# Row order of wo in its buffer, the turning of the attention quotients, and the place of the last gather, in a gated mix of cached attention and a GeGLU FFN

## The chip, the cores and the metric

The kernel runs on one core of one Trainium2 chip. The metric is device microseconds (us) of one execution; a lower number is better. A kernel is run several times and the median is compared. Beside these times one execution is recorded by the hardware profiler; its rows give start and duration of every instruction on TensorE (PE, with its weight loads as PEld), VectorE (DVE), ScalarE (ACT), GpSimd (POOL) and on the queue of SyncE (SPq), which issues all the transfers of this kernel.

## What is computed

Four decode tokens `x` (4 x 512) go through two branches that a gate mixes. Branch a is attention over a cache of 4096 keys for 32 heads of 128; branch b is a GeGLU feed-forward network of width 1792. All data is float32.

```python
g = sigmoid((x * gate_w).sum(-1, keepdims=True))
q = (x @ wq) as (4, 32, 1, 128)
scores = einsum("bhqd,bhkd->bhqk", q, k_cache) * 128 ** -0.5
o = einsum("bhqk,bhkd->bhqd", softmax(scores), v_cache)
a = o as (4, 1, 4096) @ wo                      # wo: 4096 x 512
b = (gelu(x @ w_gate) * (x @ w_up)) @ w_down    # w_down: 1792 x 512
out = g * a + (1 - g) * b
```

k_cache and v_cache are 268 MB each, and every byte is read once. wq and wo are 8.4 MB each, and the three FFN matrices 3.7 MB each.

## The kernel before

**Tiles and the loop.** The work is cut into 64 steps (`for i in range(NT)`, L311). Step i handles one pair of heads `g = i // 4` for one batch row `b = i % 4`. Its keys are one tile of 128 partitions x 32 KB (4096 KB): 64 partitions for each of the two heads, and in each partition 64 consecutive keys, so that partition p holds bytes that lie in memory right behind those of partition p-1. Its values have the same form. Five such buffers (`NB = 5`, pool `kv`) hold all large loads in turn: the two halves of wq, keys, values, w_gate, w_up, w_down and the two halves of wo (`load`, L61).

**The order of loads.** A list (L82 to L87) fixes it: keys one step ahead of values, and at the end k63, wo's first half ("w0"), v61, v62, v63 (in two halves), w_down ("d0"), and wo's second half ("w1", in three pieces of 10, 4 and 2 of its 16 blocks, `WO_END`). `load_next()` issues the next of the list on the SP queue at three places of a step: behind `sums(i)`, behind `pv(i - 1)`, and in step 62 behind `project_a(0)`. Each load waits until the buffer that it takes has been read for the last time. So k63 and w0 are issued in step 60, v61 and v62 in step 61, v63, d0 and w1 in step 62.

**A step.** VectorE multiplies the keys by the query in two halves (`products`, L192) and sums over the head's 128 elements (`sums`, L196). `max_a` (L203, L205) takes each partition's maximum and transposes it on TensorE. In the next step, between the two halves of `products`, `soft_max` reduces it (L210), spreads it by a matmul (L212), and ScalarE takes the exponentials (L217) into a zero-padded buffer. Then `pv` (L235) multiplies them by the values, 16 matmuls accumulating in PSUM over the four batch rows of a pair.

**Behind each pair.** `gather(g)` copies PSUM by ScalarE (L244), sums by four matmuls (L247), and adds the softmax's denominators by another (L249); the sums stand as 8 rows (batch, head of the pair) x 128. `weigh(g)` takes the reciprocal (L256) and writes the quotients into one of eight places of the buffer `ONA` (L257).

**Behind 8 pairs.** Once for each half of wo (step 33, and the end of the kernel) the quotients of 16 heads must become columns, with the contraction over wo's 2048 rows on 128 partitions in 16 blocks `e`. `turn(w)` does it by 32 matmuls (L265): for each of the two heads of a pair and each e, a weight block of 8 x 64 against a selecting matrix `hsel`. `turned(w)` copies the result to SBUF by ScalarE (L272). The partition that a quotient comes to is (head of the pair, k, pair): this is why wo's rows are loaded out of order. `project_a(w)` then is 64 matmuls against wo (L228), 4 for each block e; `project` places the four quarters of the output on four groups of 32 partitions.

wo's load before (L77 to L80) takes the rows of one half as `(g s e)`, with g = 8 pairs, s = 16 and e = 16, and puts row block (g, s) into partition 8 s + g. Each partition gets 16 consecutive rows, 32 KB, but neighbouring partitions of the same s lie 256 rows (512 KB) apart in memory.

**The end.** Behind the loop (L345 to L359) the order is: `soft_max(63)`, `pv(63)`, `ffn_down(0, 5)` (20 of w_down's 56 matmuls), `gather(15)`, `ffn_down(5, 9)`, `weigh(15)`, `turn(1)`, `turned(1)`, `ffn_down(9, 14)`, `project_a(1)`, the gated sum (L358), and the store of the output. Each engine works through its instructions in the order in which they are written. A fp32 matmul stands in the profile as two records, a transpose as one. The transfers of all loads go through the same queue, whose 16 DMA engines the profile shows as one share.

Of the kernel before, what the change touches and what calls it, by code (L numbers as in the profile page):

```python
# [9 lines left out]
F32 = mybir.dt.float32  # L10
AF = mybir.ActivationFunctionType
OP = mybir.AluOpType
AX = mybir.AxisListType
# [4 lines left out]
def tile_gated_mix(ctx: ExitStack, tc: tile.TileContext, x, kc, vc, wq, wo, w_gate, w_up, w_down, gate_w, out):  # L18
    nc = tc.nc
    P = 128  # L20
    B, H, S, D = kc.shape
    DM = x.shape[2]
# [3 lines left out]
    HT = 2  # L26
    PH = P // HT
# [8 lines left out]
    FC = F // P  # L36
    HW = 16
    E = HW * D // P
# [5 lines left out]
    head = ctx.enter_context(tc.tile_pool(name="head", bufs=1))  # L44
    ident = head.tile([P, P], F32)
    ones = head.tile([P, P], F32)
    sel = head.tile([P, RJ, B, HT], F32)
    hsel = head.tile([B * HT, HT, B, 8], F32)
    qd = head.tile([P, D], F32)
    xT = head.tile([P, KC, 4, B, 8], F32)  # L50
    kv = ctx.enter_context(tc.tile_pool(name="kv", bufs=NB))
    consts = ctx.enter_context(tc.tile_pool(name="consts", bufs=1))
    work = ctx.enter_context(tc.tile_pool(name="work", bufs=2))
    ps2 = ctx.enter_context(tc.tile_pool(name="ps2", bufs=2, space=PSUM))
    ps1 = ctx.enter_context(tc.tile_pool(name="ps1", bufs=1, space=PSUM))
# [5 lines left out]
    def load(kind, i):  # L61
        t = T[kind, i] = kv.tile([P, TW], F32, name="kv")
        if kind in "kv":
            h, b = HT * (i // B), i % B
            src = (kc if kind == "k" else vc)[b, h:h + HT].rearrange("h (p r) d -> (h p) (r d)", p=PH)
            n = 2 if (kind, i) == ("v", NT - 1) else 1
            for s in range(n):
                nc.sync.dma_start(t[:, s * TW // n:(s + 1) * TW // n], src[:, s * TW // n:(s + 1) * TW // n])
        elif kind == "q":
            nc.sync.dma_start(t, wq.rearrange("(p c) n -> p (c n)", c=KC)[:, i * TW:(i + 1) * TW])  # L70
        elif kind == "f":
            nc.sync.dma_start(t[:, :KC * F], (w_gate, w_up)[i].rearrange("(p c) n -> p (c n)", c=KC))
        elif kind == "d":
            nc.sync.dma_start(t[:, :FC * DM], w_down.rearrange("(p i) n -> p (i n)", i=FC))
        else:

            src = wo[i * HW * D:(i + 1) * HW * D].rearrange("(g s e) n -> s g (e n)", s=HT * D // E, e=E)  # L77
            ends = WO_END if i else (0, E)
            for e0, e1 in zip(ends, ends[1:]):
                nc.sync.dma_start(t[:, e0 * DM:e1 * DM], src[:, :, e0 * DM:e1 * DM])  # L80

    loads = [("q", 0), ("q", 1), ("k", 0)]  # L82
    for i in range(NT - 2):
# [6 lines left out]
    def load_next():  # L90
        n = next(loads, None)
        if n:
            load(*n)
# [13 lines left out]
    for j in range(RJ):  # L107
        nc.vector.tensor_reduce(sel[:, j], ident.rearrange("p (c b m) -> p b m c", c=4, b=B)[:, :, HT * j:HT * (j + 1), :],
                                axis=AX.X, op=OP.add)

    for h in range(HT):
        nc.vector.tensor_copy(hsel[:, h], ident[:B * HT, h:B * HT:HT][:, :, None].to_broadcast([B * HT, B, 8]))


    PZ = 32 - RJ * HT
# [30 lines left out]
    for c in range(KC):  # L146
        w = T["q", c // 2].rearrange("p (c n) -> p c n", c=2)[:, c % 2, :]
# [7 lines left out]
    m16 = consts.tile([P, 4 * B], F32)  # L155
    bmask = consts.tile([P, B], F32)
    amask = consts.tile([P, HG], F32)
    hmask = consts.tile([P, 4, HG], F32)
    nc.vector.tensor_reduce(m16, ident.rearrange("p (m a) -> p m a", a=HG), axis=AX.X, op=OP.add)
    nc.vector.tensor_reduce(bmask, m16.rearrange("p (j b) -> p b j", b=B), axis=AX.X, op=OP.add)  # L160
    nc.vector.tensor_reduce(amask, ident.rearrange("p (m a) -> p a m", a=HG), axis=AX.X, op=OP.add)
    nc.vector.tensor_reduce(hmask, ident.rearrange("p (j b a) -> p j a b", j=4, b=B), axis=AX.X, op=OP.add)
    for s in range(2):
# [5 lines left out]
                            op=OP.mult)  # L169
# [56 lines left out]
    def project(acc, t, w, start, stop):  # L226
        for c in range(4):
            nc.tensor.matmul(acc[32 * c:32 * c + 32, :], t, w[:, c * C4:(c + 1) * C4], start=start, stop=stop)  # L228

    def pv(i, j0=0, j1=R // RJ):  # L230
        g, b = divmod(i, B)
        N, n = RJ * D, R // RJ
        for j in range(j0, j1):
            c, m0 = j % 4, PZ + 32 * j - RJ * HT * b
            nc.tensor.matmul(PO[g % 2][32 * c:32 * c + 32].rearrange("p j d -> p (j d)"), PM[i % 2][:, m0:m0 + 32],  # L235
                             T["v", i][:, j * N:(j + 1) * N], start=b == 0 and j < 4, stop=b == B - 1 and j >= n - 4)
# [3 lines left out]
    OS, OT = {}, {}  # L240

    def gather(g):
        o = work.tile([P, RJ, D], F32, name="o", bufs=1)
        nc.scalar.activation(o, PO[g % 2], AF.Copy)  # L244
        OS[g] = ps2.tile([B * HT, D + 1], F32, name="sm")
        for j in range(RJ):
            nc.tensor.matmul(OS[g][:, :D], sel[:, j].rearrange("p b h -> p (b h)"), o[:, j, :],  # L247
                             start=j == 0, stop=j == RJ - 1)
        nc.tensor.matmul(OS[g][:, D:], RS[g % 2].rearrange("p b h -> p (b h)"), ones[:, :1], start=True, stop=True)  # L249


    ONA = consts.tile([B * HT, E, D // E, HW // HT], F32)

    def weigh(g):
        ri = work.tile([B * HT, 1], F32, name="ri")
        nc.vector.reciprocal(ri, OS[g][:, D:])  # L256
        nc.vector.tensor_scalar(ONA[:, :, :, g % (HW // HT)], OS[g][:, :D].rearrange("p (k e) -> p e k", e=E), ri, None,  # L257
                                op0=OP.mult)


    def turn(w):
        OT[w] = ps1.tile([P, E, 32], F32, name="oT")
        for h in range(HT):
            for e in range(E):
                nc.tensor.matmul(OT[w][h * PH:(h + 1) * PH, e, :], ONA[:, e].rearrange("p k g -> p (k g)"),  # L265
                                 hsel[:, h].rearrange("p b k -> p (b k)"), start=True, stop=True)

    OTS = {}

    def turned(w):  # L270
        OTS[w] = work.tile([P, E, 32], F32, name="ot", bufs=1)
        nc.scalar.activation(OTS[w], OT[w], AF.Copy)  # L272

    def project_a(w, e0=0, e1=E):
        for e in range(e0, e1):
            project(a_acc, OTS[w][:, e, :], T["w", w][:, e * DM:(e + 1) * DM], (w, e) == (0, 0),
                    (w, e) == (H // HW - 1, E - 1))

# [22 lines left out]
        for i in range(FC):  # L301
            nc.vector.transpose(hT[:, i, :], v[:, i::FC])

    def ffn_down(i0, i1):
        w = T["d", 0].rearrange("p (f n) -> p f n", n=DM)
        for f in range(i0, i1):
            project(b_acc, hT[:, f, :], w[:, f, :], f == 0, f == FC - 1)


# [1 line left out]
    for i in range(NT):  # L311
        g, b = divmod(i, B)
# [4 lines left out]
        if pair:  # L317
            weigh(g - 1)
# [9 lines left out]
        if pair and g % (HW // HT) == 0:  # L328
            turn(g // (HW // HT) - 1)
            turned(g // (HW // HT) - 1)  # L330
# [11 lines left out]
        if i == NT - 2:  # L342
            project_a(0)
            load_next()
    soft_max(NT - 1)  # L345
    pv(NT - 1)
    ffn_down(0, 5)
    gather(H // HT - 1)
    ffn_down(5, 9)
    weigh(H // HT - 1)  # L350
    turn(H // HW - 1)
    turned(H // HW - 1)
    ffn_down(9, FC)
    tb = consts.tile([P, C4], F32)
    nc.vector.tensor_scalar(tb, b_acc, g_cols[:, 1:2], None, op0=OP.mult)
    project_a(H // HW - 1)
    res = work.tile([P, C4], F32, name="res")
    nc.vector.scalar_tensor_tensor(res, a_acc, g_cols[:, 0:1], tb, op0=OP.mult, op1=OP.add)  # L358
# [23 lines left out]
```

## Time and profile before

| | |
|---|---|
| time, median of 3 runs | 1342.33 us (1341.08 to 1342.93) |
| time of the profiled execution | 1340.75 us |
| span of the profiled execution, first to last instruction | 1339.0 us |
| granted TensorE clock, mean over the span | 0.652 |
| busy: VectorE / TensorE / ScalarE | 87% / 38% / 7% of the span |
| HBM read over the span | 564.67 MB, 422 GB/s |
| DMA queue of the loads | busy for 99.5% of the span on 16 engines |

A row of a group or of the timeline names the line of the code, the engine, the operation, the written and the read tile, the shapes and the count (x). Behind it stands in brackets how long the engine had been idle and what ended that. "xN" in the timeline are N instructions drawn together. A row of stretches gives for each engine the busy time in it, then the granted TensorE clock as a share of full speed, the busy share of the DMA engines, and what they moved. Times of the timeline count from the start of the span.

### The profile page before, as it was taken

How to read it: one execution, taken by the hardware profiler on the slowest of the kernel's cores; microseconds unless marked ns; L12 is line 12 of the kernel's file. 1: busy time of each engine (PE TensorE's matmuls, PEld its weight loads, DVE VectorE, ACT ScalarE, POOL GpSimd, SP SyncE). 2: the span in 40 equal slices, each digit the busy share in tenths (PEclk: the TensorE clock that was granted, in tenths of full speed). 3: DMA queues.
4: the chain of work that ended last, by engine and by line, in shares of the span. 5: the costliest groups of instructions: out<-in, count | busy, mean ns of one | idle time of the engine just before them, and what ended most of it. 6: DMA issues, size and time to landing. Idle time of an engine off the chain costs nothing.

```text
span 1339.0 us, 7575 instructions
## 1 busy us (share of the span) xinstructions
PE 506.5 (38%) x3100; PEld 174.4 (13%) x3100; DVE 1162.4 (87%) x399; ACT 90.3 (7%) x359; POOL 0.7 (0%) x6
## 2 busy tenths in 40 slices
PE   3143334243324342443245243424433342443146
PEld 1011111011101011111022111101111110111014
DVE  2999999999997699899999999999999899999830
ACT  0000000000000000000000000000000000000000
POOL 0000000000000000000000000000000000000000
PEclk9656676676667656665675666567666666666577
DMA  9999999999999999999999999999999999999997
GB/s 407 438 423 438 435 426 437 433 429 437 432 430 437 428 435 435 427 436 434 429 436 432 430 436 433 429 438 432 430 436 430 433 434 432 432 436 431 290 396 210
DMA packets 20077, 565.15 MB, mean 422 GB/s; under 512 B 2360, under 2 KB 2376, under 8 KB 2508
## 3 DMA queue, kind: packets, MB, share of 16 engines
q1 hardware_dynamic: 20044, 564.69, 99.5%
q8 instruction: 24, 0.39, 0.1%
q14 instruction: 9, 0.07, 0.0%
HBM read 564.67 MB, written 0.01 MB: 422 GB/s over the span
## 4 chain that ended last, share of the span: by engine, by line
DMA 60%; DVE 37%; PE 2%; issue 1%; ACT 0%; SPq 0%; DVEq 0%; ACTq 0%
DMA kv<-in_A_k_cache 53%; DVE kv L192 18%; DVE sc L196 18%; DMA kv<-in_A_v_cache 3%; DMA kv<-in_A_wo 3%; DMA kv<-in_A_wq 2%; PE po L235 0%; DVE m L203 0%; PE po L151 0%; DVE m L210 0%; PE q L286 0%; PE a_acc L228 0%; DVE ONA L257 0%; PE sm L205 0%; PE q L180 0%
## 5 line engine op out<-in xcount | busy, mean ns | idle before, releaser
L192 DVE TENSOR_TENSOR kv<-kv,qb 128x4096 f32<-128x4096 f32 x128 | 564.9, 4414 | 78.4 <-DMA kv<-in_A_k_cache 76.6
L196 DVE TENSOR_REDUCE sc<-kv 128x64 f32<-128x8192 f32 x64 | 555.9, 8686 | 6.3
L235 PE MATMUL po<-kv,pm 128*32 128x512 f32 x2048 | 365.0, 877 | 297.3 <-DMA kv<-in_A_v_cache 291.4
L235 PEld LDWEIGHTS po<-kv,pm 128*32 128x32 f32 x2048 | 91.2, 154 | 515.7 <-issue 507.6
L212 PE MATMUL sm<-m,ones 1*128 1x2 f32 x128 | 37.0, 356 | 319.7 <-DVE m L210 319.7
L205 PE MATMUL sm<-ident,m 128*1 128x128 f32 x64 | 18.9, 296 | 176.6 <-DVE m L203 176.5
L212 PEld LDWEIGHTS sm<-m,ones 1*128 1x128 f32 x128 | 31.5, 304 | 351.0 <-DVE m L210 343.7
L214 ACT ACTIVATE nb<-sm 128x2 f32<-128x2 f32 x64 | 11.0, 172 | 815.3 <-PE sm L212 815.3
L217 ACT ACTIVATE pm<-sc,nb 64x64 f32<-64x64 f32 x128 | 44.6, 348 | 2.9
L210 DVE TENSOR_REDUCE m<-sm 1x2 f32<-1x128 f32 x64 | 17.4, 272 | 27.3 <-PE sm L205 27.3
L205 PEld LDWEIGHTS sm<-ident,m 128*1 128x1 f32 x64 | 5.1, 79 | 224.1 <-issue 121.1
L180 PE MATMUL q<-QM,hmask 128*64 128x512 f32 x64 | 24.3, 848 | 3.4 <-DVE QM L168 3.4
L184 ACT ACTIVATE qb<-q 128x512 f32<-128x512 f32 x16 | 9.6, 597 | 226.0 <-PE q L180 226.0
L217 ACT ACTIVATION_READ_ACCUMULATOR pm<-sc,nb 64x1 f32 x128 | 23.6, 185 | 0.0
L247 PE MATMUL sm<-o,sel 128*8 128x128 f32 x128 | 17.2, 279 | 10.7 <-ACT o L244 10.7
L244 ACT ACTIVATE o<-po 128x512 f32<-128x512 f32 x16 | 9.6, 597 | 138.5 <-PE po L235 138.5
L203 DVE TENSOR_REDUCE m<-sc 128x1 f32<-128x64 f32 x64 | 14.1, 220 | 2.2
L256 DVE RECIPROCAL ri<-sm 8x1 f32<-8x1 f32 x16 | 2.3, 147 | 15.2 <-PE sm L249 15.2
L247 PEld LDWEIGHTS sm<-o,sel 128*8 128x8 f32 x128 | 10.6, 92 | 26.8 <-ACT o L244 24.6
L151 PE MATMUL po<-kv,xT 128*32 128x512 f32 x64 | 10.9, 846 | 3.1 <-DMA kv<-in_A_wq 2.7
L164 DVE TENSOR_TENSOR u<-po,amask 128x512 f32<-128x512 f32 x2 | 1.4, 692 | 11.5 <-PE po L151 11.5
L265 PE MATMUL oT<-hsel,ONA 8*64 8x32 f32 x128 | 10.6, 257 | 0.0
(50 smaller groups left out, 88.3 us busy)
## 6 DMA issues: line engine op xcount, KB each, us to landing
kv<-in_A_k_cache SPq DMA_DIRECT2D x64, 4096.0 KB, 39.8
kv<-in_A_v_cache SPq DMA_DIRECT2D x63, 4096.0 KB, 30.6
kv<-in_A_wq SPq DMA_DIRECT2D x2, 4096.0 KB, 16.5
kv<-in_A_wo SPq DMA_DIRECT2D x1, 4096.0 KB, 53.8
kv<-in_A_v_cache SPq DMA_DIRECT2D x2, 2048.0 KB, 41.7
kv<-in_B_w_gate SPq DMA_DIRECT2D x1, 3584.0 KB, 38.6
kv<-in_B_w_up SPq DMA_DIRECT2D x1, 3584.0 KB, 28.2
kv<-in_B_w_down SPq DMA_DIRECT2D x1, 3584.0 KB, 26.0
```

What stands on the lines that cost most here:

```text
L151: nc.tensor.matmul(PO[s][32 * j:32 * j + 32].rearrange("p j d -> p (j d)"), xT[:, c, :32], w[:, n0:n0 + HB * D], start=c == 0, stop=c == K ...
L180: nc.tensor.matmul(ps[h * PH:(h + 1) * PH].rearrange("p b d -> p (b d)"), hmask[:, j, a:a + 1].to_broadcast([P, PH]), QM.rearrange("p b d ...
L192: nc.vector.tensor_tensor(t, t, QB[g][:, b:b + 1, :].to_broadcast([P, r1 - r0, D]), op=OP.mult)
L196: nc.vector.tensor_reduce(SC[i], T["k", i].rearrange("p (r d) -> p r d", d=D), axis=AX.X, op=OP.add)
L203: nc.vector.tensor_reduce(m1, SC[i], axis=AX.X, op=OP.max)
L205: nc.tensor.transpose(MT[i], m1, ident)
L210: nc.vector.tensor_reduce(m2, MT[i].rearrange("o (h p) -> o h p", h=HT), axis=AX.X, op=OP.max)
L212: nc.tensor.matmul(nbp, ones[:1, :], m2, start=True, stop=True)
L214: nc.scalar.activation(nb, nbp, AF.Copy, scale=-scale)
L217: nc.scalar.activation(PM[i % 2][:, PZ:].rearrange("p (c m) -> p c m", m=32)[s, :, h:RJ * HT:HT], SC[i][s, :].rearrange("p (c j) -> p c j" ...
L235: nc.tensor.matmul(PO[g % 2][32 * c:32 * c + 32].rearrange("p j d -> p (j d)"), PM[i % 2][:, m0:m0 + 32], T["v", i][:, j * N:(j + 1) * N], ...
L247: nc.tensor.matmul(OS[g][:, :D], sel[:, j].rearrange("p b h -> p (b h)"), o[:, j, :], start=j == 0, stop=j == RJ - 1)
```

## The change

There are three edits. wo's rows go into the buffer in their order in memory: partition p takes rows 16 p to 16 p + 15 of the half, so that the contraction's partition is (pair, head of the pair, k). For this `weigh` writes every quotient twice, once for each head of the pair (8 x 256 elements instead of 8 x 128), `turn` transposes the 8 x 128 blocks by 16 PE transposes instead of 32 matmuls, and `turned` multiplies the result by a mask that keeps in each partition the columns of its own head (`pmask`, from `m16`, once), adds the two columns, and spreads the sum to 8 equal columns by ScalarE. The two copies into `hsel` at the start go. And at the end of the kernel all of w_down's matmuls stand behind `gather`, `weigh`, `turn` and `turned`, where they stood in three parts in front of and between them.

```diff
-    hsel = head.tile([B * HT, HT, B, 8], F32)
+    t1 = head.tile([P, E * B], F32)
...
-            src = wo[i * HW * D:(i + 1) * HW * D].rearrange("(g s e) n -> s g (e n)", s=HT * D // E, e=E)
+            src = wo[i * HW * D:(i + 1) * HW * D].rearrange("(p e) n -> p (e n)", e=E)
             ends = WO_END if i else (0, E)
             for e0, e1 in zip(ends, ends[1:]):
-                nc.sync.dma_start(t[:, e0 * DM:e1 * DM], src[:, :, e0 * DM:e1 * DM])
+                nc.sync.dma_start(t[:, e0 * DM:e1 * DM], src[:, e0 * DM:e1 * DM])
...
-    for h in range(HT):
-        nc.vector.tensor_copy(hsel[:, h], ident[:B * HT, h:B * HT:HT][:, :, None].to_broadcast([B * HT, B, 8]))
...
+    pmask = consts.tile([P, HT], F32)
...
+    nc.vector.tensor_reduce(pmask, m16.rearrange("p (g h) -> p h g", h=HT), axis=AX.X, op=OP.add)
...
-    ONA = consts.tile([B * HT, E, D // E, HW // HT], F32)
+    ONA = consts.tile([B * HT, E, HW // HT, HT, D // E], F32)
...
-        nc.vector.tensor_scalar(ONA[:, :, :, g % (HW // HT)], OS[g][:, :D].rearrange("p (k e) -> p e k", e=E), ri, None,
-                                op0=OP.mult)
+        nc.vector.tensor_scalar(ONA[:, :, g % (HW // HT)],
+                                OS[g][:, :D].rearrange("p (k e) -> p e k", e=E)[:, :, None, :]
+                                .to_broadcast([B * HT, E, HT, D // E]), ri, None, op0=OP.mult)
...
     def turn(w):
-        OT[w] = ps1.tile([P, E, 32], F32, name="oT")
-        for h in range(HT):
-            for e in range(E):
-                nc.tensor.matmul(OT[w][h * PH:(h + 1) * PH, e, :], ONA[:, e].rearrange("p k g -> p (k g)"),
-                                 hsel[:, h].rearrange("p b k -> p (b k)"), start=True, stop=True)
+        OT[w] = ps1.tile([P, E, B, HT], F32, name="oT")
+        for e in range(E):
+            nc.tensor.transpose(OT[w][:, e].rearrange("p b h -> p (b h)"), ONA[:, e].rearrange("q g h k -> q (g h k)"),
+                                ident[:B * HT, :B * HT])
...
     def turned(w):
+        t = work.tile([P, E * B, HT], F32, name="tm", bufs=1)
+        nc.vector.tensor_tensor(t, OT[w].rearrange("p e b h -> p (e b) h"),
+                                pmask[:, None, :].to_broadcast([P, E * B, HT]), op=OP.mult)
+        nc.vector.tensor_tensor(t1, t[:, :, 0], t[:, :, 1], op=OP.add)
         OTS[w] = work.tile([P, E, 32], F32, name="ot", bufs=1)
-        nc.scalar.activation(OTS[w], OT[w], AF.Copy)
+        nc.scalar.activation(OTS[w].rearrange("p e (b k) -> p (e b) k", k=8), t1[:, :, None].to_broadcast([P, E * B, 8]),
+                             AF.Copy)
...
     soft_max(NT - 1)
     pv(NT - 1)
-    ffn_down(0, 5)
     gather(H // HT - 1)
-    ffn_down(5, 9)
     weigh(H // HT - 1)
     turn(H // HW - 1)
     turned(H // HW - 1)
-    ffn_down(9, FC)
+    ffn_down()
```

Nothing else of the loop, of the order of loads or of the sizes of transfers changes; wo's second half still comes in three pieces, each of all 128 partitions.

More of the change, by code (lines that the diff above doesn't have):

```diff
@@ L256, in weigh, with project_a @@
         nc.vector.reciprocal(ri, OS[g][:, D:])
-        nc.vector.tensor_scalar(ONA[:, :, :, g % (HW // HT)], OS[g][:, :D].rearrange("p (k e) -> p e k", e=E), ri, None,
-                                op0=OP.mult)
+        nc.vector.tensor_scalar(ONA[:, :, g % (HW // HT)],
+                                OS[g][:, :D].rearrange("p (k e) -> p e k", e=E)[:, :, None, :]
+                                .to_broadcast([B * HT, E, HT, D // E]), ri, None, op0=OP.mult)
     def turn(w):
-        OT[w] = ps1.tile([P, E, 32], F32, name="oT")
-        for h in range(HT):
-            for e in range(E):
-                nc.tensor.matmul(OT[w][h * PH:(h + 1) * PH, e, :], ONA[:, e].rearrange("p k g -> p (k g)"),
-                                 hsel[:, h].rearrange("p b k -> p (b k)"), start=True, stop=True)
+        OT[w] = ps1.tile([P, E, B, HT], F32, name="oT")
+        for e in range(E):
+            nc.tensor.transpose(OT[w][:, e].rearrange("p b h -> p (b h)"), ONA[:, e].rearrange("q g h k -> q (g h k)"),
+                                ident[:B * HT, :B * HT])
     OTS = {}
     def turned(w):
+        t = work.tile([P, E * B, HT], F32, name="tm", bufs=1)
+        nc.vector.tensor_tensor(t, OT[w].rearrange("p e b h -> p (e b) h"),
+                                pmask[:, None, :].to_broadcast([P, E * B, HT]), op=OP.mult)
+        nc.vector.tensor_tensor(t1, t[:, :, 0], t[:, :, 1], op=OP.add)
         OTS[w] = work.tile([P, E, 32], F32, name="ot", bufs=1)
-        nc.scalar.activation(OTS[w], OT[w], AF.Copy)
-    def project_a(w, e0=0, e1=E):
-        for e in range(e0, e1):
+        nc.scalar.activation(OTS[w].rearrange("p e (b k) -> p (e b) k", k=8), t1[:, :, None].to_broadcast([P, E * B, 8]),
+                             AF.Copy)
+    def project_a(w):
+        for e in range(E):
             project(a_acc, OTS[w][:, e, :], T["w", w][:, e * DM:(e + 1) * DM], (w, e) == (0, 0),
@@ L302, in ffn_gelu, with ffn_down @@
             nc.vector.transpose(hT[:, i, :], v[:, i::FC])
-    def ffn_down(i0, i1):
+    def ffn_down():
         w = T["d", 0].rearrange("p (f n) -> p f n", n=DM)
-        for f in range(i0, i1):
+        for f in range(FC):
             project(b_acc, hT[:, f, :], w[:, f, :], f == 0, f == FC - 1)
```

## The prediction

> **What bounds the kernel now.** I read the chain of waits first, then the costliest groups, then stretches of the end.
>
> ```profile
> DMA 60%; DVE 37%; PE 2%; issue 1%; ACT 0%; SPq 0%; DVEq 0%; ACTq 0%
> ...
> L192 DVE TENSOR_TENSOR kv<-kv,qb 128x4096 f32<-128x4096 f32 x128 | 564.9, 4414 | 78.4 <-DMA kv<-in_A_k_cache 76.6
> ```
>
> VectorE is busy, but 76.6 us of its idle time ends with keys that land: over 64 steps 1.2 us per step are left over. The loop runs at the pace of the transfers. So I ask how fast these run, in stretches (the last two columns are the DMA engines' busy share and GB/s):
>
> ```profile
> 1200.00:1245.00 45.00, 17.01 (x97) 5.32 (x89) 40.95 (x15) 2.69 (x11) 0.00 (x0) 0.69 1.01 434
> 1250.00:1275.00 25.00, 0.00 (x0) 0.00 (x0) 16.45 (x4) 0.63 (x4) 0.00 (x0) 0.50 0.99 215
> 1278.00:1290.00 12.00, 2.88 (x16) 0.91 (x20) 0.00 (x0) 0.00 (x0) 0.00 (x0) 0.50 1.01 434
> 1295.00:1309.00 14.00, 6.80 (x109) 3.43 (x97) 12.10 (x4) 1.54 (x8) 0.00 (x0) 0.87 1.02 435
> 1311.00:1329.00 18.00, 13.39 (x182) 9.60 (x178) 0.60 (x2) 0.85 (x2) 0.00 (x0) 0.78 0.95 217
> ```
>
> Twice the rate falls to half, 215 and 217 GB/s, while the engines stay busy: the queue isn't empty, its packets are slow. The issues tell what moves then. Keys land a median of 39.8 us after their issue and values 30.6 us:
>
> ```profile
> kv<-in_A_k_cache SPq DMA_DIRECT2D x64, 4096.0 KB, 39.8
> kv<-in_A_v_cache SPq DMA_DIRECT2D x63, 4096.0 KB, 30.6
> ```
>
> ```profile
> 1223.80 0.66 SPq L80 DMA_DIRECT2D kv<-in_A_wo  x1
> ...
> 1243.17 0.34 SPq L68 DMA_DIRECT2D kv<-in_A_v_cache  x1
> ...
> 1262.03 0.80 SPq L68 DMA_DIRECT2D kv<-in_A_v_cache  x2
> ...
> 1293.12 0.33 SPq L74 DMA_DIRECT2D kv<-in_B_w_down  x1
> ```
>
> w0 is issued at 1223.80, so it moves some 25 to 50 us later: the first slow stretch. The second begins when w1's turn comes. v63's halves, w_down and all keys run at 434 between. The only load with rows out of memory order is wo. What the slow stretches cost stands in the chain from 1244 us on:
>
> ```profile
> 1243.17 43.81 DMA kv<-in_A_v_cache
> ...
> 1287.12 5.94 PE po L235 x32
> ...
> 1293.27 3.63 PE a_acc L228 x128
> ...
> 1298.20 36.81 DMA kv<-in_A_wo
> ...
> 1335.06 0.69 PE a_acc L228 x16
> ```
>
> v61 waits behind w0 in the queue and lands at 1286.98. Before it nothing of step 63's softmax can go on: the transpose of step 62's maxima stands behind `pv(61)` on TensorE. At the very end the last piece of w1 is late (1298.20 + 36.81 = 1335.01), and the last 16 records of wo's matmuls end at 1335.75.
>
> **The rows of wo.** This is the large term. I take it that wo then moves at the 434 GB/s of the other loads, which have the same form (32 KB per partition, neighbours behind one another). A load of 4096 KB (4.194 MB) takes 9.66 us at 434 GB/s, one of 3584 KB 8.46 us. The start of the sum is k62's landing:
>
> ```profile
> 1244.27 4.43 DVE L192 TENSOR_TENSOR kv<-kv,qb 128x4096 f32<-128x4096 f32 x1 [0.87 <-DMA kv<-in_A_k_cache]
> ```
>
> From 1244.2 on come k63, w0, v61: three times 9.66, so v61 lands at 1273.2, 30.0 us after its issue, as the median value does (30.6). That is 13.8 us earlier than 1286.98. (Another way to the same: 25 us at 215 instead of 434 GB/s lose 12.6 us, and the edges of the stretch the rest.) v62 lands at 1282.8, v63 at 1292.5. w_down is issued when `pv(61)` ends (1279.3, now 1293.12) and w1 behind `project_a(0)`, 3.8 us later, both while the queue is still full, so w_down lands at 1301.0 and w1's last piece at 1310.6.
>
> From v61's landing to the end of `pv(63)` each link is TensorE, VectorE or ScalarE, and all move by 13.8 us: `pv(63)` ends at 1314.55 now (below) and at 1300.75 then. The values are there in time: `pv(62)` would start at about 1284.6 and needs 1282.8, `pv(63)` at 1295.8 and needs 1292.5. Minus 13.8 us.
>
> **The end behind `pv(63)`.** Now it is 21.2 us, from 1314.55 to the last matmul's end at 1335.75:
>
> ```profile
> 1309.61 4.94 PE L235 MATMUL po<-kv,pm 128*32 128x512 f32 x32 [1.18 <-ACT pm L217]
> 1314.63 0.60 ACT L244 ACTIVATE o<-po 128x512 f32<-128x512 f32 x1 [5.07 <-PE po L235]
> 1319.17 2.36 PE L228 MATMUL b_acc<-kv,hT 128*32 128x128 f32 x40 [4.61 <-DMA kv<-in_B_w_down]
> ...
> 1323.01 0.16 DVE L256 RECIPROCAL ri<-sm 8x1 f32<-8x1 f32 x1 [15.22 <-PE sm L249]
> 1323.20 0.44 DVE L257 TENSOR_SCALAR ONA<-sm,ri 8x128 f32<-8x128 f32 x1
> 1323.81 4.90 PE L265 MATMUL oT<-hsel,ONA 8*64 8x32 f32 x64
> 1328.64 2.36 PE L228 MATMUL b_acc<-kv,hT 128*32 128x128 f32 x40
> ```
>
> First 4.61 us pass until w_down lands; then w_down's parts, the gather and the turning alternate; then wo. With w_down landed at 1301.0 this wait is gone, in either order. The new chain, link by link, with rows for what hasn't been shown:
>
> ```profile
> 1222.04 1.04 PE L247 MATMUL sm<-o,sel 128*8 128x128 f32 x8 [0.71 <-ACT o L244]
> ...
> 1222.92 0.19 PE L249 MATMUL sm<-ones,rs 128*8 128x1 f32 x2
> ```
>
> ```profile
> 13.03 0.61 PE L124 MATMUL sm<-ident,x_sb 4*128 4x4 f32 x4 [13.03 <-DMA x_sb<-in_A_x]
> ```
>
> ```profile
> L164 DVE TENSOR_TENSOR u<-po,amask 128x512 f32<-128x512 f32 x2 | 1.4, 692 | 11.5 <-PE po L151 11.5
> L272 ACT ACTIVATE ot<-oT 128x512 f32<-128x512 f32 x2 | 1.2, 597 | 31.6 <-PE oT L265 31.6
> L124 PE MATMUL sm<-ident,x_sb 4*128 4x4 f32 x4 | 0.6, 254 | 13.0 <-DMA x_sb<-in_A_x 13.0
> L355 DVE TENSOR_SCALAR tb<-b_acc,g_cols 128x128 f32<-128x128 f32 x1 | 0.3, 350 | 7.4 <-PE b_acc L228 7.4
> ```
>
> - Copy by ScalarE: 0.74 us with its handovers.
> - Sums: 1.07 us inside the loop (1222.04 to 1223.11); I take 1.3 for a slower clock, at most 1.8.
> - Reciprocal and quotients: 0.83 now (1323.01 to 1323.81 and a handover of 0.03). 128 more elements cost by L164 against L355 (342 ns for 384 elements) 0.12 us, at most another 0.44; I take 0.98 in all.
> - 16 transposes: the trace has four like them (L124, weights of 128 columns), 254 ns each and (0.61 - 0.254) / 3 = 0.12 us apart; 15 x 0.12 + 0.25 = 2.05 us, where 64 records took 4.90. Bounds: 1.2 (77 ns apart, as L265's) to 4.1 (one after the other).
> - Mask, sum, ScalarE's copy: 0.35 + 0.25 + 0.60 and three handovers, 1.35 us, beside w_down's matmuls (3.2 us at least, below). Without that cover it would be 1.35 us more.
> - 112 records for w_down and 128 for wo, back to back. A record takes 59 ns at half clock (2.36 / 40) and 28.9 at full (3.70 / 128):
>
> ```profile
> 1293.20 3.70 PE L228 MATMUL a_acc<-kv,ot 128*32 128x128 f32 x128
> ```
>
> ```profile
> 1312.40:1319.00 6.60, 2.16 (x20) 0.36 (x12) 0.00 (x0) 0.60 (x1) 0.00 (x0) 1.00 0.98 217
> 1319.20:1322.40 3.20, 3.20 (x46) 2.61 (x47) 0.00 (x0) 0.00 (x0) 0.00 (x0) 0.50 1.03 241
> 1322.60:1325.90 3.30, 3.30 (x77) 3.06 (x75) 0.60 (x2) 0.00 (x0) 0.00 (x0) 1.00 0.94 207
> 1326.00:1332.70 6.70, 6.70 (x104) 6.33 (x106) 0.35 (x1) 0.60 (x1) 0.00 (x0) 0.50 0.69 195
> ```
>
> The third column from the end is the granted clock. It is full from 1312.4, 2.8 us into `pv(63)`; half through 1322.4, the first 3.3 us of w_down's matmuls; half again through the turning until 1332.7, 4.1 us into the next dense run. So I take half clock for 3.5 us: 59 records, then 181 x 28.9 ns = 5.2, together 8.7 us. Bounds: 7.0 (all full) and 14.2 (all half).
>
> Sum: 0.74 + 1.3 + 0.98 + 2.05 + 8.7 = 13.8 us instead of 21.2. TensorE ends at 1314.5; the last piece of w1 (1310.6) is 3.3 us ahead of the 16 records that need it. Minus 7.4 us. Behind the last matmul nothing changes (3.25 us, from 1335.75 to the span's end).
>
> **What costs nothing.** In step 33 the mask and the sum stand on VectorE in front of the products of step 34, and wait for the transposes:
>
> ```profile
> 700.13 5.68 PE L265 MATMUL oT<-hsel,ONA 8*64 8x32 f32 x64
> ...
> 700.66 4.43 DVE L192 TENSOR_TENSOR kv<-kv,qb 128x4096 f32<-128x4096 f32 x1 [0.78 <-DMA kv<-in_A_k_cache]
> ```
>
> The transposes would run from 700.13 to 702.2, the products start at 702.9 instead of 700.66, 2.2 us late, once; two steps with 1.2 us to spare take it up, and later issues only thin a queue that is 30 us deep. The 16 wider quotients are 0.12 to 0.44 us each, in steps with 1.2 us to spare. Uncovered, both would be 2.2 + 16 x 0.12 = 4.1 us. `hsel` and `pmask` at the start lie beside the wait for wq.
>
> **Total:** 13.8 + 7.4 = 21.2 us. Against the profiled execution (span 1339.0, time 1340.75) this gives 1317.8 and 1319.55; its time lies 1.58 us under the median of the runs, so against 1342.33 it is 1321.1 us.
>
> **Rivals.**
> - *Loads share the engines* and don't go in order, so that v61 lands with v62, at 1282.8: 4.2 + 7.4 = 11.6 us, 1330.7. Against it speak the steady 30.6 and 39.8 us of values and keys issued 0.4 us apart: one whole load between them. 0.06.
> - *wo gets only part of the rate*, say 325 GB/s (12.9 us a load): v61 3.2 us later, w1 lands at 1317.1, 1324.4. 0.05.
> - *The row order isn't what halves the rate* (it is where wo lies, or how it is cut). Then w1's last piece still lands at 1335.01, and the shorter work behind `pv(63)` only waits for it: 1342.3, no change. For it: no run here has loaded wo otherwise. Against it: w_down, an equally small matrix, and the 2048 KB halves run at 434. 0.06. The Trainium skill has a rule on that, in "DMA: Bandwidth & Descriptors", section "Latency and other measured facts": a row pitch of 512 KiB between partitions, which is wo's here, gave copies 207 GB/s where 214 was their full rate, and only pitches from 2 MiB on were much slower. By it the old order would lose 3%, an estimate of 0.6 us for both halves of wo, and the cause would be another; this trace, with 215 against 434, doesn't fit that figure, though no run here has yet parted the pitch from the rest. The same row advises laying tiles out contiguously.
> - *The new order is slower still*: the 16 engines read in it from places 256 KB apart instead of 32 KB, and if that suits wo worse, w1's last piece ends later than now. It decides below 201 GB/s (8.39 MB in 41.7 us instead of 39.0, the 2.7 us of a measurable loss); at 145 GB/s the end is 18.9 us later, 1361. Against it: keys and values are read so at 434. 0.04.
>
> **How the numbers follow.** Forecast 0.79. With the low bounds the sum behind `pv(63)` is 10.7 us, but then w1 binds (1310.6 + 0.69): 24.4 us in all, 1317.9, and I allow 1.5 us below for the landing and the median. With the high bounds it is 22.1 us (0.74 + 1.8 + 1.27 + 4.1 + 14.2): 12.9 us in all, 1329.4. The range 1316.4 to 1329.4 takes in forecast and part of the rate, 0.84. About 0.2% (2.7 us) is what a measurement tells from no change here. Faster 0.90, same 0.06, slower 0.04.
>
> **What would show it.** No stretch from 1245 us on under 420 GB/s until the loads run out near 1311 us; v61's `pv` starting near 1273 and `pv(63)` ending near 1301; no wait for w_down or for wo on TensorE; 16 transposes in about 2 us; VectorE late once, near 703 us, with nothing behind it late. I am wrong if the 215 GB/s stay, if values still end the wait at 1287, or if the end behind `pv(63)` is over 17 us.

## The result and the profile after

The changed kernel takes 1317.36 us (median of 6 runs, 1316.97 to 1318.03) where the kernel before takes 1342.32 (median of 6). The ratio is 0.9815, with a 95% interval of 0.9803 to 0.9828: 25.0 us less, where 21.2 had been forecast. The profiled execution took 1317.39 us, its span is 1315.5 us.

Stretches of the changed kernel (GB/s last, the DMA engines' share before it, the granted TensorE clock before that). The first is the one that stood at 215 GB/s; the second is the time in which wo's first half moves, the third that of wo's second half in its pieces (by the bytes that are left, the first 2 us of it still belong to w_down; from 1298.5 to 1304 us alone it is 413 GB/s). The last two are `pv(63)` and the end behind it, and show the granted clock:

```profile
1250.00:1275.00 25.00, 1.72 (x10) 0.50 (x14) 16.36 (x4) 0.54 (x4) 0.00 (x0) 0.50 1.01 435
1253.00:1263.00 10.00, 0.00 (x0) 0.00 (x0) 9.86 (x4) 0.00 (x0) 0.00 (x0) 0.50 1.00 433
1296.00:1304.00 8.00, 6.86 (x42) 2.00 (x34) 0.34 (x2) 0.60 (x1) 0.00 (x0) 0.69 0.97 415
1295.40:1301.00 5.60, 5.60 (x28) 1.34 (x32) 0.00 (x0) 0.00 (x0) 0.00 (x0) 0.50 0.94 401
1301.10:1312.20 11.10, 9.62 (x274) 8.39 (x266) 1.49 (x5) 1.23 (x2) 0.00 (x0) 1.00 0.64 269
```

While loads are queued, no stretch stands at half rate any more; in the last one the loads run out, and the DMA engines' share falls with the rate. The chain of waits of the same execution, from v61 on:

```profile
1243.10 30.04 DMA kv<-in_A_v_cache
1273.14 0.14 issue
1273.28 5.53 PE po L233 x32
...
1283.77 8.70 DVE sc L194
...
1295.35 6.49 PE po L233 x32
1301.84 0.02 issue
1301.87 0.60 ACT o L242
1302.47 0.04 issue
1302.52 1.04 PE sm L245 x8
...
1303.81 0.48 DVE ONA L256
1304.29 0.04 issue
1304.34 1.17 PE oT L264 x16
1305.51 3.19 PE b_acc L226 x112
1308.70 3.54 PE a_acc L226 x128
1312.24 0.03 issue
1312.27 0.35 DVE res L360
```

v61 lands at 1273.14 instead of 1286.98. Behind it there is no further transfer in the chain: the last one before the end, 36.81 us of wo in the kernel before, is gone from it, and TensorE ends at 1312.24 instead of 1335.75.

### The profile page after: what moved, and what is told of

The parts are those of the page before. It is cut to its first block, busy times and chain, and to the rows that moved or that the text cites. A ratio compares the mean times of both kernels' runs of the same rounds, so it can differ in the third digit from the quotient of the medians.

```text
span 1315.5 us, 7385 instructions
## 1 busy us (share of the span) xinstructions
PE 500.1 (38%) x3004; PEld 164.5 (13%) x3004; DVE 1165.0 (89%) x402; ACT 90.5 (7%) x359; POOL 0.7 (0%) x6
## 2 busy tenths in 40 slices
DMA packets 20076, 565.14 MB, mean 430 GB/s; under 512 B 2360, under 2 KB 2376, under 8 KB 2508
## 4 chain that ended last, share of the span: by engine, by line
DMA 61%; DVE 36%; PE 2%; issue 1%; ACT 0%; SPq 0%; DVEq 0%; ACTq 0%
DMA kv<-in_A_k_cache 58%; DVE sc L194 17%; DVE kv L190 17%; DMA kv<-in_A_v_cache 2%; PE po L233 1%; DVE m L201 0%; DVE m L208 0%; PE q L290 0%; PE a_acc L226 0%; DVE ONA L256 0%; PE b_acc L226 0%; PE oT L264 0%; PE sm L203 0%; PE q L178 0%; DVE hT L306 0%
## 5 line engine op out<-in xcount | busy, mean ns | idle before, releaser
L233 PE MATMUL po<-kv,pm 128*32 128x512 f32 x2048 | 372.2, 892 | 283.6 <-DMA kv<-in_A_v_cache 277.7
```

## The experiments

My theory at the start was the prediction's: the order of wo's rows halved the rate of the transfers, and the new order brings it back. Rivals were that the turning or the order of the end brings the gain, and that wo is slow for another reason.

**Only the load, in the kernel before.**

```diff
-            src = wo[i * HW * D:(i + 1) * HW * D].rearrange("(g s e) n -> s g (e n)", s=HT * D // E, e=E)
+            src = wo[i * HW * D:(i + 1) * HW * D].rearrange("(p e) n -> p (e n)", e=E)
...
-                nc.sync.dma_start(t[:, e0 * DM:e1 * DM], src[:, :, e0 * DM:e1 * DM])
+                nc.sync.dma_start(t[:, e0 * DM:e1 * DM], src[:, e0 * DM:e1 * DM])
```

> The kernel before with one edit: wo's rows are loaded in memory order (the rows then don't match the quotients' order, so the attention branch's projection is another sum; its work is the same). Theory, that the order of the rows halves the transfer rate: no stretch under 420 GB/s from 1245 us on, v61's wait ends near 1273 us instead of 1287, TensorE ends 13.0 to 17.7 us behind pv(63) (40 records, sums, 64 turning records of 4.9 us, 200 records), so 1320 to 1325 us. Rival, that wo is slow for where it lies or how it is cut: 215 GB/s stay and the time is 1341 to 1343 us. Rival, that the turning brings the gain: also 1341 to 1343 us.

Measured: 1319.42 us, ratio 0.9837 (0.9821 to 0.9853). That is 22.5 us of the whole gain from this edit alone. The stretch of wo's first half, then its chain of waits, v61 and from `pv(63)` on:

```profile
1253.00:1263.00 10.00, 0.00 (x0) 0.00 (x0) 9.86 (x4) 0.00 (x0) 0.00 (x0) 0.50 1.01 436
```

```profile
1243.12 30.07 DMA kv<-in_A_v_cache
...
1295.26 6.37 PE po L235 x32
1301.63 1.09 PE b_acc L228 x40
1302.72 0.86 PE sm L247 x8
...
1304.51 3.96 PE oT L265 x64
1308.48 2.29 PE b_acc L228 x40
1310.77 3.75 PE a_acc L228 x128
1314.52 0.03 issue
```

`pv(63)` ends about where it does in the changed kernel (1301.63), and the end behind it takes 12.9 us, where it took 21.2 before and takes 10.4 in the changed kernel. So 8.3 of the 10.8 us that the end has lost come from the load too: w_down and wo have landed when TensorE wants them. The theory stands against both rivals, but this run doesn't yet part the order of the rows from the form of the source pattern, which changes with it. 1319.42 lies just under the 1320 to 1325 expected; of the records for w_down and wo only the 40 at 1308.48 ran at half clock (2.29 us).

**Only the load put back, in the changed kernel.**

```diff
-            src = wo[i * HW * D:(i + 1) * HW * D].rearrange("(p e) n -> p (e n)", e=E)
+            src = wo[i * HW * D:(i + 1) * HW * D].rearrange("(g s e) n -> s g (e n)", s=HT * D // E, e=E)
...
-                nc.sync.dma_start(t[:, e0 * DM:e1 * DM], src[:, e0 * DM:e1 * DM])
+                nc.sync.dma_start(t[:, e0 * DM:e1 * DM], src[:, :, e0 * DM:e1 * DM])
```

> The changed kernel with one edit: wo's rows are loaded in the old order (rows and quotients don't match; the work is the same). Theory, that the order of the rows halves the rate: 215 GB/s again while wo moves, the last piece of w1 lands near 1335 us, 1340 to 1343 us although turning and tail are the new ones. Rival, that turning or the tail's order bring the gain: 1318 to 1330 us.

Measured: 1341.8 us, ratio 0.9998 (0.9988 to 1.0008). Its chain waits for v61 and then for wo, as in the kernel before:

```profile
1243.21 43.73 DMA kv<-in_A_v_cache
...
1295.92 34.13 DMA kv<-in_A_wo
1330.05 0.14 issue
1330.18 5.65 PE a_acc L226 x128
1335.84 0.02 issue
```

Turning and order of the end are worth nothing while wo moves at half rate: TensorE ends at 1335.84, as at 1335.75 before.

**What about the load is slow.** A source pattern is a list of steps, each with a count. The kernel before has two steps, 16 groups (the outer count) of 8 partitions each; memory order has one step, taken 128 times. Four kernels fill wo's buffer from other addresses, with the same number of bytes (in some, rows are read more than once); each was run once. In the first two, `ga` is the step in blocks of 32 KB from one group of eight partitions to the next and `gb` the step within a group (the kernel before has 1 and 16, memory order is 8 and 1):

```diff
-            src = wo[i * HW * D:(i + 1) * HW * D].rearrange("(p e) n -> p (e n)", e=E)
+            ga, gb = ((8, 16), (1, 1))[i]
+            src = type(wo)(tensor=wo.tensor, offset=wo.offset, ap=[[ga * E * DM, P // 8], [gb * E * DM, 8], [1, E * DM]])
...
```

> The changed kernel; only the addresses that wo is read from differ (other rows than the reference's, the same bytes and packets). The first half is read with 8 blocks of 32 KB (256 KB) from one group of eight partitions to the next and 16 blocks (512 KB) from partition to partition within a group; the second half with 1 block (32 KB) for both steps. Theory, that reading streams clash that stand 32 KB apart: first half at 434 GB/s, v61's wait ends near 1273 us; second half at about 215, its last piece some 10 us later than 1310, about 1327 us in all. Rival, that the 512 KB step within the group is it: first half at 215, v61's wait ends near 1287; second half at 434; about 1331 us. Rival, that any pattern with two steps is slow: both at 215, about 1341 us.

The second kernel differs from the first in one line:

```diff
...
+            ga, gb = ((1, 8), (2, 16))[i]
...
```

> The changed kernel; only the addresses that wo is read from differ (other rows than the reference's, the same bytes and packets). The first half is read with 1 block (32 KB) from group to group of eight partitions and 8 blocks (256 KB) within a group; the second half with 2 blocks (64 KB) from group to group and 16 blocks (512 KB) within. Theory, that streams 32 KB apart clash: first half at about 215 GB/s, v61's wait ends near 1287 us; second half between 215 and 434, as 64 KB are better or not. Rival, that the 512 KB step within the group is it: first half at 434, v61's wait ends near 1273; second half at 215. Rival, that any pattern with two steps is slow: both at 215, about 1341 us.

Measured: 1340.71 and 1342.65 us. The stretch in which wo's first half moves, then the one of the second; first for the steps 8, 16 and 1, 1:

```profile
1253.00:1263.00 10.00, 0.00 (x0) 0.00 (x0) 9.86 (x4) 0.00 (x0) 0.00 (x0) 0.50 1.00 216
1313.00:1323.00 10.00, 8.31 (x134) 5.91 (x130) 1.14 (x4) 1.23 (x2) 0.00 (x0) 0.84 0.94 218
```

and for the steps 1, 8 and 2, 16:

```profile
1253.00:1263.00 10.00, 0.00 (x0) 0.00 (x0) 9.86 (x4) 0.00 (x0) 0.00 (x0) 0.50 0.97 203
1313.00:1323.00 10.00, 7.49 (x102) 4.33 (x98) 1.15 (x4) 1.23 (x2) 0.00 (x0) 0.84 0.96 216
```

All four patterns, with the outer count 16, give half rate, whatever the steps are. Both explanations by addresses that I had set against each other (streams 32 KB apart, or steps of 512 KB) fall, and the rival that I had named last stays: the form of the pattern. The next kernel parts form and addresses. Its first half is read nearly in memory order, but with two steps; its second half with one step of 512 KB, from the key cache:

```diff
-            src = wo[i * HW * D:(i + 1) * HW * D].rearrange("(p e) n -> p (e n)", e=E)
+            if i == 0:
+                src = type(wo)(tensor=wo.tensor, offset=wo.offset, ap=[[9 * E * DM, P // 8], [E * DM, 8], [1, E * DM]])
+            else:
+                src = type(kc)(tensor=kc.tensor, offset=kc.offset, ap=[[16 * E * DM, P], [1, E * DM]])
...
```

> The changed kernel; only the addresses that wo's buffer is filled from differ (other rows than the reference's, and for the second half the key cache; the same bytes and packets). The first half is read almost in memory order but in a pattern with two steps: 288 KB from group to group of eight partitions, 32 KB within. The second half is read in a pattern with one step, of 512 KB from each partition to the next. Theory, that the pattern's form (16 groups of 8 partitions) is slow and the addresses don't matter: first half at 215 GB/s, v61's wait ends near 1287 us; second half at 434 GB/s, in all about 1331 us. Rival, that addresses matter (512 KB steps, or streams close together): first half at 434, v61's wait ends near 1273; second half at 215 or less, 1327 us or more.

Measured: 1331.39 us, with 213 GB/s for the nearly ordered half and 424 for the half with 512 KB from partition to partition:

```profile
1253.00:1263.00 10.00, 0.00 (x0) 0.00 (x0) 9.86 (x4) 0.00 (x0) 0.00 (x0) 0.50 1.01 213
1310.00:1319.00 9.00, 6.89 (x52) 2.60 (x53) 0.63 (x2) 1.16 (x5) 0.00 (x0) 0.79 0.99 424
```

So it is not where the rows lie. This fits the figure that the prediction had weighed against the change, in the Trainium skill's "DMA: Bandwidth & Descriptors", section "Latency and other measured facts": a pitch of 512 KiB gave copies 207 GB/s, with 214 as the full rate. Here it costs nothing that shows: 424 against 415 for the same pieces in memory order, and 412 against 413 where the stretches hold wo's pieces alone (1313 to 1319 us here, 1298.5 to 1304 us there).

Last, the writing side and the outer count, again with one run each. One kernel loads wo's first half in memory order by two transfers of 64 partitions each:

```diff
+            if i == 0:
+                for h in range(2):
+                    nc.sync.dma_start(t[h * PH:(h + 1) * PH], src[h * PH:(h + 1) * PH])
+                return
```

> The changed kernel with wo's first half loaded by two transfers, of partitions 0 to 63 and 64 to 127, each with one step and in memory order; the result is the reference's. Theory, that what halves the rate is on the writing side (at any time only half of the buffer's partitions are written to, in the slow pattern by the way the 16 engines divide it): about 215 GB/s while it moves, v61's wait ends near 1287 us, about 1331 us in all. Rival, that the cause is in how a pattern with two steps is read or made: 434 GB/s throughout, v61 near 1273, about 1317 us.

The other keeps two steps, with the outer count 128 for the first half and 32 for the second:

```diff
+            if i == 0:
+                src = type(wo)(tensor=wo.tensor, offset=wo.offset, ap=[[17 * DM, P], [9 * DM, 2], [1, 8 * DM]])
+            else:
+                src = type(wo)(tensor=wo.tensor, offset=wo.offset + 5 * E * DM, ap=[[5 * E * DM, 32], [E * DM, 4], [1, E * DM]])
...
```

> The changed kernel; only the addresses that wo is read from differ (other rows than the reference's, the same bytes). The first half is read in a pattern with two steps whose outer count is 128 partitions, and in each partition two runs of 16 KB with a gap of 2 KB; the second half in one with outer count 32 (groups of four partitions, 160 KB apart, 32 KB within). Theory, that the outer count of 16 divides the partitions badly among the engines: first half at 434 GB/s, v61's wait ends near 1273 us; the second half full or half, as groups of four are dealt out. Rival, that any pattern with two steps is slow: first half at 215, v61's wait ends near 1287; second half at 215; about 1341 us in all.

Measured: 1332.75 us for the partition halves, with 213 GB/s while they move:

```profile
1253.00:1263.00 10.00, 0.00 (x0) 0.00 (x0) 9.86 (x4) 0.00 (x0) 0.00 (x0) 0.50 1.04 213
```

and 1317.23 us for the outer counts 128 and 32, both at full rate:

```profile
1253.00:1263.00 10.00, 0.00 (x0) 0.00 (x0) 9.86 (x4) 0.00 (x0) 0.00 (x0) 0.50 1.03 444
1296.00:1304.00 8.00, 6.71 (x42) 2.00 (x34) 0.49 (x2) 0.60 (x1) 0.00 (x0) 0.70 0.99 423
```

Shown is this: a load of 128 partitions x 32 KB runs at half rate when its source has two steps with the outer count 16, and at full rate with one step or with the outer counts 32 (wo's second half, in its pieces) or 128; and a load of 64 partitions at a time in memory order runs at the same half rate. It is neither smaller packets (20077 before, 20076 in the changed kernel) nor engines without work (their share is 0.94 to 1.04 in the slow stretches). Outer count and size of a group change together in these patterns, so the runs don't tell the one from the other. The Trainium skill's "SBUF — State Buffer", section "Door 1: The DMA port swizzle", says that 64 partitions reach only 8 of the buffer's 16 ports. The 213 GB/s of the partition halves agree. What it suggests for the outer count 16 is only argued: that the 16 engines then take eight neighbouring partitions each and so write, in step, into half of the ports at a time. The trace doesn't tell which engine reads or writes which partition, so that stays open, and so do the 256 KB between the engines' places that the prediction's last rival works with.

**The order of the end.** The changed kernel again, and two versions in which w_down's matmuls stand in three parts: blocks 0 to 4, 5 to 8 and 9 to 13 as before, and 0 to 1, 2 to 5 and 6 to 13.

> The changed kernel itself, beside the two versions of its end in this call. Every theory: 1317.4 us within half a microsecond, pv(63) about 6.4 us long or shorter by up to 1.5 us, as the clock's step from half to full falls.

```diff
...
+    ffn_down(0, 5)
     gather(H // HT - 1)
+    ffn_down(5, 9)
     weigh(H // HT - 1)
     turn(H // HW - 1)
     turned(H // HW - 1)
-    ffn_down()
+    ffn_down(9, FC)
```

> The changed kernel with one edit undone: w_down's matmuls stand again in three parts, 5 blocks in front of the gather, 4 between it and the quotients, 5 behind the turning. Theory, that w_down has landed by then and TensorE is idle in the changed kernel only while ScalarE copies (0.65 us) and VectorE makes the quotients (0.8 us): the parts fill these gaps, 9.1 us behind pv(63) instead of 10.4, about 1316.1 us. Rival, that the gather first is what shortens the end: 0.5 to 1.2 us longer, about 1318 us. Rival, that w1's last piece binds either way: 1317.4 us.

```diff
...
+    ffn_down(0, 2)
     gather(H // HT - 1)
+    ffn_down(2, 6)
     weigh(H // HT - 1)
     turn(H // HW - 1)
     turned(H // HW - 1)
-    ffn_down()
+    ffn_down(6, FC)
```

> The changed kernel with w_down's matmuls in three parts cut to the gaps: 2 blocks in front of the gather (0.46 us beside the copy of 0.65), 4 between it and the quotients (0.93 us beside 0.8), 8 behind the turning (1.9 us beside mask, sum and copy of 1.3). Theory of the gaps: 9.3 us behind pv(63), about 1316.2 us, as the version with 5, 4 and 5 blocks or better by 0.1. Rival, that the gather first is what shortens the end: over 1317.4 us. Rival, that w1's last piece binds: 1317.4 us.

Measured: 1317.07, 1317.13 and 1316.95 us, with ratios 0.9815 (0.9802 to 0.9829), 0.9815 (0.9802 to 0.9829) and 0.9814 (0.9800 to 0.9827): no difference. The theory of the gaps, which expected 1316.1 and 1316.2 us, failed. The ends of the chains say why. The changed kernel again, from its timeline; behind it the version with the parts as before and the one with small parts, from their chains:

```profile
1295.90 4.97 PE L233 MATMUL po<-kv,pm 128*32 128x512 f32 x32 [1.19 <-ACT pm L215]
...
1311.24 0.65 PE L226 MATMUL a_acc<-kv,ot 128*32 128x128 f32 x16 [0.40 <-DMA kv<-in_A_wo]
```

```profile
1283.38 27.65 DMA kv<-in_A_wo
1311.02 0.17 issue
1311.20 0.68 PE a_acc L226 x16
```

```profile
1283.95 26.97 DMA kv<-in_A_wo
1310.91 0.16 issue
1311.07 0.68 PE a_acc L226 x16
```

In all three the last 16 records wait for w1's last piece, which lands at 1310.9 to 1311.0. So the rival that this piece binds was right, and the gaps that the parts fill are filled for nothing. In the first of the three it binds by a hair: TensorE ends the 112 records in front at 1310.85, the piece lands at 1310.86, and 0.39 us more pass until the first of the 16 starts.

## Why the prediction was right

- **The rate of wo's loads.** The size of the step was right: v61 at 1273.14, forecast 1273.2; 13.8 us, as worked out. What it rested on was half wrong. The prediction named the rows' order in memory ("the only load with rows out of memory order is wo"), and its rival of the steps within wo named addresses as well. The runs show the count of the outer step instead. So the rival that the row order isn't the cause was true in its first half; its consequence, no change, failed, because the change removes the second step together with the order; a change that had only reordered the addresses would have gained nothing, as the nearly ordered half at 213 GB/s suggests. In that the forecast was lucky: the edit that was to mend the order took the second step away with it.
- **From v61 to the end of `pv(63)`.** Forecast 1300.75; 1301.84 in the first profile and 1300.87 in the second. The difference is `pv(63)` itself, 6.49 and 4.97 us: in the first it ran at half clock up to 1301.0 (the stretch at 0.50 above), in the second only up to 1298.9 (0.54 before it, 1.00 behind). Both are the same program.
- **The end behind `pv(63)`.** Forecast 13.8 us, 10.4 in the first profile. The mis-sized terms: 240 records took 6.73 us instead of 8.7, as the clock stayed full from 1301.1 to 1312.2 through the copy, the quotients and the transposes, where I had put half clock for 3.5 us; sums 1.08 instead of 1.3, for the same reason; the transposes 1.17 us instead of 2.05; quotients 0.74 instead of 0.98. The clock doesn't explain the transposes: the four of L124 that they were sized from also ran at full clock (1.00 from 12.9 to 14.0 us), 0.12 us apart, and the 16 in a row came 73 ns apart. Records and transposes came out just under their low bounds (7.0 and 1.2 us), and so did the end, 10.4 against 10.7; from the low bounds as they are listed that sum is 10.8. Nor did w_down run at 434 GB/s to its end in the kernel before, as the prediction has it: it landed at 1319.1 us, 8 us into the second slow stretch. That the end shrinks by itself was half right: the kernel with only the load changed shows that 8.3 us of it come from the load. The turning adds 2.3 us (1319.42 against 1317.13 with turning and load changed and the parts as before), and the new order of w_down's matmuls nothing.
- **Which limit binds.** "The last piece of w1 is 3.3 us ahead": it was not. It landed as forecast (1310.7 in the first profile, forecast 1310.6), but TensorE was faster than forecast, and in the second profile it stands idle for 0.40 us before the 16 records, which start at 1311.24. With the end at both limits, a shorter `pv(63)` (1.5 us less there) moves the span only from 1315.5 to 1315.1.
- **Step 33.** Forecast 2.2 us late, once. The products of step 34 started at 702.46 instead of 700.66, and the idle time for keys was back two steps later:

```profile
701.99 0.29 DVE L271 TENSOR_TENSOR tm<-oT,pmask 128x128 f32<-128x128 f32 x1 [2.09 <-PE oT L264]
702.31 0.22 DVE L273 TENSOR_TENSOR t<-tm 128x64 f32<-128x64 f32 x1
702.46 4.42 DVE L190 TENSOR_TENSOR kv<-kv,qb 128x4096 f32<-128x4096 f32 x1
```

```profile
720.35 4.42 DVE L190 TENSOR_TENSOR kv<-kv,qb 128x4096 f32<-128x4096 f32 x1
...
739.41 4.42 DVE L190 TENSOR_TENSOR kv<-kv,qb 128x4096 f32<-128x4096 f32 x1 [1.07 <-DMA kv<-in_A_k_cache]
```

  The products of step 35 follow at once on what stands before them, those of step 36 wait for their keys again. v61 was issued at 1243.10, where it had been 1243.17. The wider quotients take 472 ns instead of 438.
- **The total.** 1321.1 forecast, 1317.36 measured. 2.3 us are TensorE's earlier end (1312.24 instead of 1314.5); the rest is about the 1.58 us by which the profiled execution of the kernel before lay under its median, which I had carried over and which the changed kernel doesn't show (1317.39 against 1317.36).

## What to carry to other kernels

Look at the rate in stretches beside the DMA share: here a queue that was busy at half the usual GB/s was a load whose form was wrong, not one that came too late, and the slow time was longer than this load alone would have taken. Before a source pattern with two steps is used for a wide load, try another outer count or one step, even if the layout then has to be mended by a few small instructions on engines that have time. And when a fast transfer frees the end of a kernel, ask what lands last then: here the transfers' own end binds again, and reordering matmuls in front of it is worth nothing.

## What the runs showed of the hardware that I had not expected

- Loads of the same size from wo move at 203 to 220 GB/s with two steps and the outer count 16, and at 423 to 444 with the outer counts 32 and 128; the distance of the rows in memory (32 KB to 512 KB) showed no effect.
- Two transfers of 64 partitions, in memory order and queued one behind the other, move at 213 GB/s, like the slow pattern.
- A slow load costs more than its own time: in the kernel before, 25 us at 215 GB/s moved 5.4 MB, more than the 4.2 MB of wo's half, so at least 1.2 MB of the loads around it moved at that rate too. v61 landed 13.8 us late, where 4.2 MB at half rate alone would lose 9.8 (4.194 MB at 215 instead of 434 GB/s). How the neighbours are slowed isn't shown.
- The same instructions of `pv(63)` took 4.97 and 6.49 us in two executions of one program, as the granted clock went from half to full at 1298.9 us in the one and behind 1301.0 us in the other.
